# One core, attention and a feed-forward layer: the order of issue read from a written list in place of a list scheduler

## The chip, the cores and the metric

The kernel runs on one core of a Trainium2 chip. The metric is the device time of one execution in microseconds (us). Three runs of the kernel before took 973.44, 973.48 and 976.46 us. Differences within about 0.3% of the time (some 2.9 us) can't be told from no change by a few runs.

## The reference

```python
def phi(x):                       # x is q or k, scaled by 64 ** -0.25; omega is 128 x 64
    proj = einsum('bhsd,md->bhsm', x, omega)
    sq = sum(x * x, axis=-1, keepdims=True) / 2
    h = proj - sq
    return exp(h - max(h, axis=-1, keepdims=True)) / sqrt(128)
q_p, k_p = phi(q), phi(k)         # 8 batches x 8 heads, 576 rows, 64 wide
kv = einsum('bhsm,bhsd->bhmd', k_p, v)
z = sum(k_p, axis=2)
attn = einsum('bhsm,bhmd->bhsd', q_p, kv) / (einsum('bhsm,bhm->bhs', q_p, z)[..., None] + 1e-6)
x = attn as 4608 tokens x 512
h = x @ w_in                      # 512 x 2048
g = h * erf(softplus(h))
out = g @ w_out                   # 2048 x 512
```

## The kernel before

Everything is fp32. A matrix product of the feed-forward layer is three matmuls: each operand is split into a high part (`xh`, `wh`, `gh`, `th`, `bh`, ...) and a rest (`xl`, `wl`, `gl`, `tl`, `bl`, ...), and high x high, high x rest and rest x high are added up in one bank of PSUM.

The 64 heads are taken as 32 pairs. A pair is called `_b_p` (batch, pair); the steps of one are: load (`uk`, `uq`, or `x` and `y`, and `v`), square for the norm (`sqk`, `sqq`, `square`, `sumsq`, the last `s<-y` in the profile), project (banks `ppk`, `ppq`, or `pm`, `p0k`, `p0q`, `p1k`, `p1q`), maximum (`mx..`, `pm<-...`), exponential (`fk`, `fq`), sum keys with values (`kvp`, copied to `kh`), turn q round (PE transposes into `pt`, three copies `qh<-pt` called `turnhigh`; from pair 20 on through DRAM, stored as `dq` by `qstore` and read back as `qh` by four `qfetch`), multiply (`nd`), and divide (`y<-nd,rc`). The quotient `y` has one buffer. Nine or so small transfers (`yfetch`, `xs<-y` in the profile) carry it to the tokens' layout, and the next pair's `divide` may write `y` only when the last of them has landed.

The feed-forward layer runs over six groups of tokens ("supers"): two of 2 x 288 tokens with plain products, and four of 2 x 432 tokens, where the blocks are multiplied in seven products instead of eight (tables `PRODUCTS`, banks `hX`, `hY`, `hZ` for the first product and `oX`, `oY`, `oZ` for the second). Each bank is emptied several times into sums in SBUF: first by a copy (`hout` into `hs`, `oout` into `os`), then by additions (`hadd`, `oadd`, on DVE). `xsum` (`xc<-xs,..`) and `xrest` (`xl<-xc,xh`) make the operands of the first product, `gsum` (`gs<-hs`), `gate` (`hs<-gs,hs`), `high` (`th<-gs`, `bh<-hs`) and `rest` (`tl<-gs,th`) those of the second. Attention for later tokens is woven between the products of earlier ones, so that PE always has something to do.

What each step does, and what it must wait for, is written in `build`, which makes 4661 steps (`Op`). Many can go to more than one engine: copies to ACT or DVE, a gate or a rest to POOL or DVE. `Plan.order` plays the program through with estimated costs, picks for every idle engine the ready step that is due first (a table `DATES` of number and offset, indexed by the step's number, moves the due times), and returns the steps in the order in which they start, each with an engine (`o.eng`) and its buffers (`t.slot`). The loop at the end of `tile_attention_moe` emits them in that order. Each engine, and the DMA queue that SP issues, then carries out its own instructions strictly in the order in which they were emitted. All instructions have line L1523 in the profile, since one helper records them.

## Time and profile before

| | |
|---|---|
| median of 3 runs | 973.48 us |
| span of the profiled execution (first to last instruction) | 970.2 us |
| median less span: start and end around it | 3.3 us |
| PE busy, its weight loads (PEld) | 954.5 us, 903.8 us |
| DVE, ACT, POOL busy | 761.5, 625.4, 583.4 us |
| matmuls | 7868 |
| moved by DMA | 255.64 MB |

The profile is of one execution; its own total time isn't on the page, so the span stands for it and the 3.3 us are taken as fixed. Engines: PE multiplies, DVE, ACT and POOL do the elementwise work, SP issues the DMAs (rows with SPq). The kernel is one engine's work with small gaps, so what matters is where PE stands still and which engine released it. A row of a timeline that ends in "x36" is a run of 36 instructions of one kind, and its second number is the time of the whole run.

### The profile page before, as it was taken

The numbers are of one execution on the slowest core, as the hardware profiler recorded it, in microseconds if no ns is written. First come the engines' busy times: TensorE is split into PE (matmuls) and PEld (weight loads), VectorE is DVE, ScalarE is ACT, GpSimd is POOL, SyncE is SP. The second block draws the span as 40 slices with busy tenths as digits, with TensorE's granted clock in tenths as the row PEclk, the third lists the DMA queues.
The fourth block names the chain that finished last, engine by engine and source line by source line (L and its number), as shares of the span: only waits on it lengthen the run. The fifth ranks groups of instructions, "written<-read, shape, count | busy, mean of one in ns | idle before, by whom it ended". The sixth has DMA issues, their size and how long they took to land.

```text
span 970.2 us, 20988 instructions
## 1 busy us (share of the span) xinstructions
PE 954.5 (98%) x7868; PEld 903.8 (93%) x7868; DVE 761.5 (78%) x1161; ACT 625.4 (64%) x1157; POOL 583.4 (60%) x416
## 2 busy tenths in 40 slices
PE   8999999999999999999998999999999999999998
PEld 8899999999999999999998999888999999999997
DVE  6879788767777977768797879789898699668674
ACT  7869787875866766665476375666747547564650
POOL 3234534947747666748496758388686486548620
PEclk9999999999999999999999999999999999999999
DMA  8667779598897798897898999998998776697651
GB/s 250 213 212 235 236 258 329 206 329 317 309 282 227 254 322 285 257 316 232 272 316 249 385 294 322 288 301 262 292 307 248 249 243 219 215 309 220 222 184 74
DMA packets 116388, 255.64 MB, mean 263 GB/s; under 512 B 14272, under 2 KB 31168, under 8 KB 116288
## 3 DMA queue, kind: packets, MB, share of 16 engines
q1 hardware_dynamic: 116128, 254.24, 79.9%
q8 instruction: 63, 1.03, 0.4%
q14 instruction: 37, 0.30, 0.1%
q10 hardware_dynamic: 160, 0.07, 0.0%
HBM read 194.74 MB, written 50.07 MB: 252 GB/s over the span
## 4 chain that ended last, share of the span: by engine, by line
PE 56%; DMA 4%; DVE 4%; SPq 0%; ACT 0%; issue 0%; DVEq 0%; ACTq 0%
PE hX L1523 13%; PE oX L1523 11%; PE hY L1523 7%; PE o L1523 7%; PE oY L1523 5%; PE hZ L1523 4%; PE oZ L1523 3%; DMA wb<-wdc 2%; PE kvp L1523 2%; PE nd L1523 1%; PE p0k L1523 1%; PE p1k L1523 1%; DMA y<-xN 1%; DMA xs<-y 1%; DMA wb<-wdw 1%; DVE os L1523 1%
## 5 line engine op out<-in xcount | busy, mean ns | idle before, releaser
L1523 POOL TENSOR_TENSOR hs<-gs,hs 128x864 f32<-128x864 f32 (+1 forms) x56 | 111.2, 2012 | 112.0 <-ACT gs L1523 82.8
L1523 PE MATMUL o<-gh,w 128*128 128x288 f32 (+1 forms) x704 | 167.4, 317 | 0.0
L1523 PE MATMUL hX<-xh,wb 128*128 128x432 f32 x512 | 161.6, 361 | 1.8 <-DVE y L1523 1.4
L1523 PEld LDWEIGHTS o<-gh,w 128*128 128x128 f32 x704 | 120.8, 188 | 2.1
L1523 PE MATMUL h<-xh,w 128*128 128x288 f32 x512 | 110.6, 300 | 0.0
L1523 PE MATMUL o<-gl,w 128*128 128x288 f32 (+1 forms) x352 | 110.0, 312 | 0.0
L1523 PEld LDWEIGHTS hX<-xh,wb 128*128 128x128 f32 x512 | 96.1, 188 | 7.9 <-issue 1.8
L1523 ACT ACTIVATE hs<-hX 128x432 f32<-128x432 f32 x65 | 34.7, 533 | 104.0 <-PE hX L1523 103.2
L1523 PE MATMUL oX<-th,wb 128*128 128x432 f32 x312 | 97.4, 360 | 2.2 <-DVE os L1523 2.2
L1523 PE MATMUL hX<-xl,wb 128*128 128x432 f32 x256 | 91.8, 359 | 0.0
L1523 ACT ACT_TABLE_LOAD x67 | 86.0, 1283 | 2.1 <-PEq L1908 0.7
L1523 PE MATMUL hY<-xh,wb 128*128 128x432 f32 x256 | 84.0, 363 | 1.2 <-ACT fk L1523 0.4
L1523 PEld LDWEIGHTS h<-xh,w 128*128 128x128 f32 x512 | 84.2, 188 | 0.9 <-ACT fk L1523 0.2
L1523 PE MATMUL h<-xl,w 128*128 128x288 f32 x256 | 75.4, 295 | 0.0
L1523 DVE TENSOR_TENSOR os<-oX,os 128x432 f32<-128x432 f32 x86 | 50.9, 600 | 24.5 <-PE oX L1523 24.3
L1523 ACT ACTIVATE gs<-hs 128x1728 f32<-128x1728 f32 (+1 forms) x48 | 69.4, 1483 | 0.4
L1523 ACT ACTIVATE gs<-gs 128x1728 f32<-128x1728 f32 (+1 forms) x48 | 69.1, 1480 | 0.3
L1523 PEld LDWEIGHTS o<-gl,w 128*128 128x128 f32 x352 | 66.3, 188 | 0.9
L1523 PEld LDWEIGHTS oX<-th,wb 128*128 128x128 f32 x312 | 58.6, 188 | 5.9 <-DVE os L1523 2.9
L1523 POOL TENSOR_TENSOR bl<-hs,bh 128x864 fp32r<-128x864 f32 x22 | 57.5, 2634 | 0.0
L1523 PE MATMUL oX<-tl,wb 128*128 128x432 f32 x156 | 55.9, 359 | 0.0
L1523 POOL TENSOR_TENSOR tl<-gs,th 128x864 fp32r<-128x864 f32 x20 | 44.5, 2246 | 18.8 <-ACT th L1523 13.9
(162 smaller groups left out, 2699.9 us busy)
## 6 DMA issues: line engine op xcount, KB each, us to landing
wb<-wdc SPq DMA_DIRECT2D x232, 256.0 KB, 4.6
wb<-wdw SPq DMA_DIRECT2D x174, 256.0 KB, 4.8
w<-wdw SPq DMA_DIRECT2D x44, 512.0 KB, 6.1
st<-w SPq DMA_DIRECT2D x32, 512.0 KB, 5.7
wdw<-w SPq DMA_DIRECT2D x32, 512.0 KB, 4.7
wdc<-c SPq DMA_DIRECT2D x32, 512.0 KB, 5.9
x<-xR SPq DMA_DIRECT2D x20, 576.0 KB, 6.5
y<-xN SPq DMA_DIRECT2D x20, 576.0 KB, 6.3
```

Of the source, the lines that this page charges most:

```text
L1523: return tc.keep_in_program_order(method(*args, **kwargs))
```

## The change

`Plan.order` no longer schedules. It reads `ORDER`, a string of 4661 items, in the order in which they are emitted: the step's number, a letter where the step could go to several engines (T is PE, A ACT, V DVE, G POOL, S SP; without one the step takes its first option), and after a colon the buffers, one hexadecimal digit each. The costs, lags and the table `DATES` are gone. The steps, their names and what each depends on are the same 4661 as before; 390 of them change engine, and the order changes on all engines. PE has the same 7868 matmuls, SP the same 890 transfers, ACT the same 67 table loads. The other edits of the diff are new options (`TWIN`, `SUMG`, `LENT`, `BOTH` as a set), which are set so that the same steps result. All instructions now have line L1211.

```diff
-    def order(self, slots, caps):
-        ops = self.ops
...
-        for i, x in DATES:
-            ops[i].due += x
...
-                    o.eng, o.start = e, now
-                    for t in o.alloc:
-                        t.slot = free[t.pool].pop(0)
...
+    def order(self):
+
+        out, table = [], "exp"
+        for item in ORDER.split():
+            item, _, slots = item.partition(":")
+            o = self.ops[int(item.rstrip("TAVGS"))]
+            o.eng = item[-1] if item[-1] in "TAVGS" else o.opts[0][0]
+            for i, t in enumerate(o.alloc):
+                t.slot = int(slots[i], 16) if slots else 0
+            if o.eng == "A" and o.set is not None and o.set != table:
+                if o.set == "exp":
+                    out.append("table")
...
-DATES = ((0, -155.4), (1, 0.9), (2, -0.7), (4, -446.6), (5, -58.8), (6, -11.2), (7, -171), (8, -17.9),
...
+ORDER = """
...
+39:2 35A 38:1 40 42:0 47:2 49:3 41 83:3 155G 51:4 43 48V:4 52V 50A 168A 53:56 208 207:7 60:2 54V
...
+3004 3005 3103:1 3039:5 3020 3054 3040 3006 3035 3007 3041A 2882G 3016:42 3010 3036A:3 3018 3011
...
+3274 3099A:1 3275 3317:376 3333 3257A 3252A 3265 3334:0 3271 3093V 3094G 3313 3319A 3282 3318V 3283
...
-    for o in plan.order(slots, CAPS):
+    for o in plan.order():
```

The numbers that the text comes back to: 48, 50 and 52 are the three copies `qh<-pt` of the first pair (before, 48 and 50 on DVE and 52 on ACT). 3041, 3257 and 3481 are `hout` copies of banks `hY`, `hX` and `hY` (before on DVE, in the list 3041A, 3257A and 3481A).

**ACT near 30 us.** The rows of ACT before, from the exponentials of the keys of the third pair (`fk_2`) to the next q copy (`qh_2`). The name before the arrow is what is written, the last number only tells buffers apart; `uq_3` is the square for the fourth pair's q, `wt` and `w` prepare a weight, `fq_2` are the exponentials of the third pair's q.

```order
L1523 ACTIVATE fk_2_387<-ppk_2_0_333,mxk_2_351 128x128 x3
L1523 ACTIVATE fk_2_387<-ppk_2_2_356,mxk_2_351 128x128 x3
L1523 ACTIVATE fk_2_387<-ppk_2_1_347,mxk_2_351 128x128 x3
L1523 ACTIVATE uq_3_371<-uq_3_371 64x1152
L1523 ACTIVATE wt_0_2_464<-st_0_2_196 128x512
L1523 ACTIVATE w_0_1_2_194<-wt_0_1_306 128x2x256
L1523 ACTIVATE fq_2_479<-ppq_2_0_420,mxq_2_462 128x128 x3
L1523 ACTIVATE fq_2_479<-ppq_2_2_438,mxq_2_462 128x128 x3
L1523 ACTIVATE fq_2_479<-ppq_2_1_428,mxq_2_462 128x128 x3
```

The same place on ACT in the change:

```order
L1211 ACTIVATE fk_2_362<-ppk_2_2_357,mxk_2_355 128x128 x3
L1211 ACTIVATE fk_2_362<-ppk_2_1_346,mxk_2_355 128x128 x3
L1211 ACTIVATE wt_0_2_426<-st_0_2_208 128x512
L1211 ACTIVATE rc_1_435<-nd_1_0_395,eps 128x5
L1211 ACTIVATE w_0_1_2_203<-wt_0_1_299 128x2x256
L1211 ACTIVATE fq_2_450<-ppq_2_0_419,mxq_2_438 128x128 x3
L1211 ACTIVATE fq_2_450<-ppq_2_1_431,mxq_2_438 128x128 x3
L1211 ACTIVATE fq_2_450<-ppq_2_2_444,mxq_2_438 128x128 x3
```

The square of `uq_3` is no longer between the two rounds of exponentials (it is now on POOL), and a small `rc` has come in.

**DVE near 660 us.** The rows of DVE before, while PE multiplies into the `o` banks of the fourth super. `os<-oX`, `os<-oY` and `os<-oZ` empty the banks that PE waits for, `s_1` is a `sumsq` for a later pair, `xl` and `xc` are the `xrest` and `xsum` of the next super's tokens.

```order
L1523 TENSOR_TENSOR os_2_7583<-oX_2_0_8573,os_2_7583 128x432
L1523 TENSOR_TENSOR os_0_7529<-oY_2_0_8645,os_0_7529 128x432
L1523 TENSOR_REDUCE s_1_8715<-y_1_8351 128x18
L1523 TENSOR_TENSOR xl_0_8641<-xc_0_8275,xh_0_8571 128x1728
L1523 TENSOR_TENSOR os_3_7650<-oY_2_1_8722,os_3_7650 128x432
L1523 TENSOR_TENSOR os_3_7650<-oX_2_1_8581,os_3_7650 128x432
L1523 TENSOR_TENSOR xc_1_8739<-xs_1_1_7509,xs_0_1_7032 128x432
L1523 TENSOR_TENSOR xc_1_8739<-xs_1_1_7509,xc_1_8739 128x432
L1523 TENSOR_TENSOR os_1_7571<-oY_2_1_8722,os_1_7571 128x432
```

The same place on DVE in the change (`pm` and `mx` are the maximum's last steps):

```order
L1211 TENSOR_TENSOR os_2_7577<-oX_2_0_8552,os_2_7577 128x432
L1211 TENSOR_TENSOR os_1_7564<-oX_2_1_8564,os_1_7564 128x432
L1211 TENSOR_TENSOR os_3_7696<-oY_2_1_8703,os_3_7696 128x432
L1211 SCALAR_TENSOR_TENSOR pm_1_8627<-s_1_8576,pm_1_8627 128x18
L1211 SCALAR_TENSOR_TENSOR mx_1_8725<-s_1_8576,pm_1_8627 128x18
L1211 TENSOR_TENSOR xl_0_8596<-xc_0_8248,xh_0_8587 128x1728
L1211 TENSOR_TENSOR os_1_7564<-oY_2_1_8703,os_1_7564 128x432
L1211 TENSOR_TENSOR os_2_7577<-oX_2_0_8552,os_2_7577 128x432
L1211 TENSOR_TENSOR os_3_7696<-oX_2_1_8564,os_3_7696 128x432
L1211 TENSOR_TENSOR xc_1_8764<-xs_0_1_7019,xs_0_0_6988 128x432
```

The drain `os_3<-oY_2_1` now stands ahead of the long `xl`, and the `sumsq` is gone from between (it stands some twenty rows earlier).

**SP near 515 us.** The DMA issues of SP before, around the four reads of q for pair `_5_2` (`qh_2<-dq_2`) and the transfers of the quotient of pair `_5_0` (`xs_0<-y_0`); `wb` are weights, `y_0<-xN` a load.

```order
L1523 DMA wb_6965<-wdw_0_6_7_1065 128x512
L1523 DMA xs_0_0_6982<-y_0_6643 32x2x288 x2
L1523 DMA xs_0_0_6982<-y_0_6643 32x2x144
L1523 DMA qh_2_7002<-dq_2_6934 32x4x288 x4
L1523 DMA y_0_7018<-xN 128x1152
L1523 DMA wb_7025<-wdc_0_2_1_3446 128x512
L1523 DMA wb_7025<-wdc_0_3_1_3636 128x512
L1523 DMA xs_0_1_7032<-y_0_6643 32x2x144 x3
L1523 DMA xs_0_0_6982<-y_0_6643 32x2x288 x2
L1523 DMA xs_0_1_7032<-y_0_6643 32x2x144
L1523 DMA xs_0_0_6982<-y_0_6643 32x2x144 x2
L1523 DMA wb_7074<-wdc_0_2_0_3407 128x512
```

The same place on SP in the change:

```order
L1211 DMA wb_6963<-wdw_0_6_7_1064 128x512
L1211 DMA xs_0_0_6988<-y_0_6667 32x2x288
L1211 DMA xs_0_0_6988<-y_0_6667 32x2x144
L1211 DMA xs_0_0_6988<-y_0_6667 32x2x288
L1211 DMA xs_0_0_6988<-y_0_6667 32x2x144
L1211 DMA xs_0_0_6988<-y_0_6667 32x2x288
L1211 DMA y_0_7007<-xN 128x1152
L1211 DMA xs_0_0_6988<-y_0_6667 32x2x288
L1211 DMA xs_0_1_7019<-y_0_6667 32x2x144 x3
L1211 DMA wb_7033<-wdc_0_2_1_3415 128x512
L1211 DMA qh_2_7039<-dq_2_6954 32x4x288 x4
L1211 DMA xs_0_0_6988<-y_0_6667 32x2x144 x2
```

The reads of q stand behind six more of the quotient's transfers, the load of `y_0` and one weight; the last transfer of the quotient is now followed by fewer weights (one more `xs_0_1` comes behind the rows shown, ahead of the weight `wb_7074`).

## Rows read from the trace of the kernel before

**Rows 1.** The page, span and busy time of each engine.

```profile
span 970.2 us, 20988 instructions
PE 954.5 (98%) x7868; PEld 903.8 (93%) x7868; DVE 761.5 (78%) x1161; ACT 625.4 (64%) x1157; POOL 583.4 (60%) x416
```

**Rows 2.** Busy time by stretch: us; busy (instructions) per engine; clock, DMA share, GB/s.

```profile
0.00:57.00 57.00, 52.48 (x672) 48.21 (x673) 43.18 (x98) 43.77 (x137) 21.98 (x27) 1.00 0.74 215
500.00:680.00 180.00, 173.65 (x1433) 158.82 (x1433) 151.40 (x221) 113.49 (x229) 129.03 (x84) 1.00 0.93 299
```

**Rows 3.** Two windows of 25 us, columns PE, PEld, DVE, ACT, POOL as before.

```profile
650.00:675.00 25.00, 23.03 (x128) 20.89 (x127) 24.02 (x31) 17.63 (x18) 19.86 (x14) 1.00 0.91 276
875.00:900.00 25.00, 25.00 (x129) 23.93 (x128) 19.89 (x20) 10.45 (x13) 19.45 (x9) 1.00 0.71 223
```

**Rows 4.** Timeline near 15 us: start, us, engine, operation [idle before <-releaser].

```profile
13.04 1.16 ACT L1523 ACTIVATE uk<-uk 64x1152 f32<-64x1152 f32 x1 [1.16 <-DMA uk<-kT]
15.28 1.89 PE L1523 MATMUL nd<-kh,qh 128*64 128x65 f32 x35 [1.31 <-DVE qh L1523]
```

**Rows 5.** Timeline near 30 us, ACT and PE.

```profile
29.20 1.16 ACT L1523 ACTIVATE uq<-uq 64x1152 f32<-64x1152 f32 x1 [2.31 <-DMA uq<-qT]
31.41 2.43 ACT L1523 ACTIVATE fq<-ppq,mxq 128x128 f32<-128x128 f32 x9
32.34 0.55 PE L1523 MATMUL pt<-ident,fq 128*128 128x128 f32 x3 [0.63 <-ACT fq L1523]
33.37 1.17 PE L1523 MATMUL pt<-ident,fq 128*128 128x128 f32 x6 [0.49 <-ACT fq L1523]
```

**Rows 6.** Timeline near 587 us, DVE and PE.

```profile
584.78 2.19 DVE L1523 TENSOR_TENSOR gs<-hs 128x864 f32<-128x864 f32 x1
587.54 0.47 PE L1523 MATMUL hY<-xh,wb 128*128 128x432 f32 x1 [0.36 <-DVE hs L1523]
```

**Rows 7.** Timeline near 600 us, DVE, POOL and PE.

```profile
597.15 4.96 DVE L1523 TENSOR_TENSOR tl<-gs,th 128x1728 fp32r<-128x1728 f32 x1
598.11 2.19 POOL L1523 TENSOR_TENSOR gs<-hs,gs 128x432 f32<-128x432 f32 x2
609.29 0.46 PE L1523 MATMUL oX<-th,wb 128*128 128x432 f32 x1 [0.97 <-DVE os L1523]
```

**Rows 8.** Timeline from 651 to 666 us, DVE and PE.

```profile
651.40 2.08 DVE L1523 TENSOR_TENSOR tl<-gs,th 128x1728 fp32r<-128x1728 f32 x1
...
659.51 1.94 DVE L1523 TENSOR_TENSOR xl<-xc,xh 128x1728 fp32r<-128x1728 f32 x1
...
662.02 0.47 PE L1523 MATMUL oY<-bh,wb 128*128 128x432 f32 x1 [1.28 <-DVE os L1523]
...
665.07 0.46 PE L1523 MATMUL oZ<-bh,wb 128*128 128x432 f32 x1 [0.45 <-DVE os L1523]
```

**Rows 9.** Timeline from 513 to 534 us: SP's issues, PE and DVE.

```profile
513.79 3.98 SPq L1523 DMA_DIRECT2D qh<-dq  x4
...
525.43 1.22 PE L1523 MATMUL nd<-kh,qh 128*64 128x65 f32 x36
...
527.96 0.60 SPq L1523 DMA_DIRECT2D xs<-y  x1
...
531.01 0.82 DVE L1523 TENSOR_TENSOR y<-nd,rc 128x320 f32<-128x320 f32 x2 [3.90 <-DMA wb<-wdw]
...
531.65 0.44 PE L1523 MATMUL hX<-xh,wb 128*128 128x432 f32 x1 [1.42 <-DVE y L1523]
...
533.71 0.47 PE L1523 MATMUL oX<-th,wb 128*128 128x432 f32 x1 [1.23 <-DVE os L1523]
```

**Rows 10.** DMA issues from 508 to 523 us: issue, count, KB each, median us to landing.

```profile
qh<-dq SPq DMA_DIRECT2D x4, 144.0 KB, 6.1
```

**Rows 11.** Timeline of PE near 536.7 us: into the projection of x.

```profile
536.58 0.36 PE L1523 MATMUL hX<-xh,wb 128*128 128x432 f32 x1
536.87 0.37 PE L1523 MATMUL p0k<-wr,x 64*128 64x128 f32 x1
```

More of the change, by code (lines that the diff above doesn't have):

```diff
@@ L336 @@
-DATES = ((0, -155.4), (1, 0.9), (2, -0.7), (4, -446.6), (5, -58.8), (6, -11.2), (7, -171), (8, -17.9),
[439 rows of a table removed]
+    def order(self):
[9 more added lines that the diff above has]
+                    out.append("table")
+                table = o.set
+            out.append(o)
+        return out
@@ L785 @@
 ROWS = 20
-BOTH = 12
+BOTH = frozenset(range(12, 32))
+TWIN = False
+SUMG = frozenset()
+LENT = 3
 SUMA = ()
@@ L1203, in attention @@
             load(0, "q")
-        if n < BOTH:
+        if n not in BOTH:
             project(n, "q", 0.15)
         if n + 1 < N:
-            if n + 1 < BOTH:
+            if n + 1 not in BOTH:
                 load(n + 1, "k")
@@ L1218, in attention @@
         if n + 1 < N:
-            if n + 1 < BOTH:
+            if n + 1 not in BOTH:
                 project(n + 1, "k", 0.0)
@@ L1665, in project_mid, with project_rows @@
             pe.matmul(b.ap[:, :2 * P], lhsT=x.ap[:, (NC - 1) * P:], rhs=wr, start=True, stop=True)
-        def project_rows(self, banks, x, i):
-            for c in range(4):
-                for z, b in enumerate(banks):
-                    r, k = slice(z * D, (z + 1) * D), 4 * i + c
-                    pe.matmul(b.ap[:, c * P:(c + 1) * P], lhsT=x.ap[r, k * P:(k + 1) * P],
-                              rhs=wr[r, z * P:(z + 1) * P], start=True, stop=True)
+        def project_rows(self, banks, x, i, twin, head):
+            jobs = [[(banks[j][z], c, 4 * j + c) for j in range(2) for c in range(4)] for z in range(2)]
+            if twin:
+                jobs[0].insert(0, (banks[2][0], 0, NC - 1))
+                jobs[1].append((banks[2][1], 1, NC - 1))
+            cut = 4 + twin
+            for two in list(zip(*jobs))[i * cut:][:cut]:
+                for z, (b, c, k) in enumerate(two):
+                    r = slice(z * D, (z + 1) * D)
+                    m = pe.matmul(b.ap[:, c * P:(c + 1) * P], lhsT=x.ap[r, k * P:(k + 1) * P],
+                                  rhs=wr[r, z * P:(z + 1) * P], start=True, stop=True)
+                    if z and k == NC - 1:
+                        tc.add_manual_dep(m.ins, head[0].ins.name, mybir.DependencyInfo(
+                            mybir.DependencyClass.Sync, mybir.DependencyReason.DATA), reason="one bank")
         def raw(self, mid):
```

499 lines of the change are left out of this document (306 added, 193 removed), and 439 rows, old and new, of the table DATES.

## The prediction

> **What bounds the kernel now.** I read the page's head first: PE is busy 954.5 of 970.2 us, and no other engine is above 78% [rows 1]. So the time is PE's work plus its gaps, and since the change leaves PE the same 7868 matmuls, only the gaps, 970.2 - 954.5 = 15.7 us, are open to it. Busy DVE or POOL time matters only where PE waits behind it.
>
> Next I looked where the gaps lie, by stretches. Up to 57 us PE is idle 57.00 - 52.48 = 4.5 us, and from 500 to 680 us it is idle 180.00 - 173.65 = 6.35 us [rows 2]. These two stretches hold 10.9 of the 15.7 us; most of the rest lies behind the last matmul, where the last sums are stored, and that work doesn't change. A window at 875 us has no gap at all, one at 650 us has 1.97 us, and there DVE is busy 24.02 of 25 us [rows 3].
>
> Last I took the waits in the two stretches one by one, and read on the waking engine what stood ahead of the instruction that PE wanted. Near 15 us PE waits 1.31 us for a q copy; ACT, which makes the third of the three copies, is held by a square of 1.16 us [rows 4]. Near 32 us it waits 0.63 and 0.49 us for exponentials of q; ACT had first waited 2.31 us for a load and then squared it for 1.16 us, and the exponentials begin at 31.41 [rows 5]. At 587.54 PE waits 0.36 us for an `hY` drain on DVE that stands behind a gsum of 2.19 us [rows 6]; the same pattern comes twice more before 680 us, three waits in all and about 1.0 us together. At 609.29 it waits 0.97 us for an `os` drain, on a DVE that is late since a rest took 4.96 us [rows 7]. At 662.02 and 665.07 it waits 1.28 and 0.45 us for drains behind an xrest of 1.94 us [rows 8]. And near 531 us two waits of 1.42 and 1.23 us follow the divide into `y` at 531.01, which had to wait until the last `xs<-y`, issued at 527.96, had landed [rows 9].
>
> **The change part by part.** *Start.* Of the three q copies of the first pair, 50 moves to ACT, 48 and 52 are on DVE, and the square at 13.04 leaves ACT. The last copy then no longer waits for ACT's square. The nd wait can't vanish, since three copies on two engines still take two turns of 0.5 us; I take half of 1.31, 0.6 us, between 0 and 1.3. The square of `uq_3` moves to POOL, so the exponentials near 31.41 need not wait 2.31 + 1.16 us [rows 5]: both pt waits go, 1.1 us (0 if the new `rc`, which needs an nd of PE, comes late; it stands ahead of the exponentials on ACT). The first loads stand in another order, with v and a part of q ahead of two parts of the keys. The nearest row is an issue of 0.60 us [rows 9]; two of them are 0 to 1.2 us, and I take 0.3, near the lower end, since only the first pair's maxima and exponentials follow at once. Start: -0.6 - 1.1 + 0.3 = -1.4 us.
>
> *Drains.* 3041, 3257 and 3481 go from DVE to ACT and no longer stand behind a gsum: -1.0 us (0 if ACT is itself late there; it has room, 113.49 of 180 us [rows 2]). The rest of 4.96 us moves to POOL, and the wait at 609.29 behind it goes: -0.97 (0 if the maxima that stay on DVE hold it up). Near 660 us the drain `os_3<-oY_2_1` goes ahead of the xrest and the sumsq is moved twenty rows up: -1.28 - 0.45 = -1.73 (bounded by 0, as one long xrest still stands ahead of the next drain, `os_1<-oY_2_1`). Drains: -3.7 us.
>
> *The place at 531 us.* Here two things go against each other. The last transfer of the quotient is issued about two weights earlier, but PE now comes to the banks of `nd` sooner: it has 6 product matmuls and pm ahead of `p0k`, where it had 15 and pm ahead of hX. Nine matmuls at 25.00 / 129 = 0.194 us [rows 3] are 1.7 us less cover. So the first wait stays and may grow by about what the second, 1.23 us, saves. Also, the four reads of q go behind six more `xs`, a load and a weight. The six alone are 6 x 0.60 = 3.6 us, with two shorter issues some 4.4 us. Their last issue ends at 513.79 + 3.98 = 517.8 and takes 6.1 us to land [rows 9, 10], 523.9 against nd at 525.43; so 1.5 us of slack stands against 4.4, and nd may wait 2.9 us, with p0k, pm and the products queued behind it on PE. That wait overlaps the divide's, since the divide is held by the landing of `xs`, not by nd. I take 0 for the place; its ends are -2.6 (both waits gone) and +2.9.
>
> *Refilling PE.* The first matmul after each wait takes 0.46 or 0.47 us where one in the stream takes 0.36 [rows 7, 8, 11]; eight waits fewer are 8 x 0.1 = -0.8 us.
>
> *Switching PE.* The row-wise projections now come in 24 groups in place of 21. Going in costs 536.87 - 536.58 = 0.29 us from start to start in place of 0.194 [rows 11, 3]; with as much on the way out it is 0.2, for three groups +0.6 us.
>
> *The other moves.* 390 steps change engine. Between 500 and 680 us ten steps go from POOL to DVE (three rests and two gates among them) and seven back, and sixteen each way between DVE and ACT. A rest takes DVE 2.08 to 4.96 us [rows 8, 7]. Net four rests and gates more on DVE are 8.3 us at the shorter price; three gsums at 2.19 us [rows 6] leave it, 6.6 us. With the small steps, most of which cancel, I take 2 to 6 us more, so up to 157 of 180. PE waits for none of it as long as the drains are first in line. I cost it at nothing; what it costs when that cover is gone is the second rival.
>
> Sum: -1.4 - 3.7 + 0 - 0.8 + 0.6 = -5.3 us. Against the profiled execution that is a span of 970.2 - 5.3 = 964.9; with the 3.3 us around it, which put it at the median of 973.5, 968.2 us.
>
> **Rivals.** *The waits only move.* Every drain has a neighbour that is nearly as late: in the window at 650 us DVE has 0.98 us of 25 free [rows 3], and a reordering on a full engine makes another bank late. For it speaks that DVE gets more work in that very stretch, against it that ACT and POOL have room (113.49 and 129.03 of 180 us [rows 2]) and take the drains. If all of the stretch's 6.35 us stay and only the start's 1.4 us comes, the time is 973.5 - 1.4 + 0.6 = 972.7, at most 975.6 with the 2.9 us of nd: no difference that can be measured (970.6 to 976.4).
>
> *DVE becomes the bound from 500 to 680 us (slower).* A rest on DVE took 4.96 us at 597.15, while POOL worked beside it from 598.11, and 2.08 us at 651.40 [rows 7, 8]: the same instruction, 2.88 us apart. If the five rests and gates that move to DVE there all meet POOL, that is 5 x 2.88 = 14.4 us more; with the 2 to 6 us, 168 to 172 of the 173.65 us that PE works. DVE is then as full everywhere as it is now in the window at 650 us, where PE loses 1.97 us in 25 [rows 3]. Over 180 us that is 14.2 us in place of 6.35, so 973.5 + 7.8 - 1.4 = 979.9 us. It decides from about 24 of 25 busy DVE microseconds on; below that the drains find room. Against it: POOL is busy 129.03 of 180 us there [rows 2], and drops work that goes to DVE, so not every one of the five meets it. The Trainium skill has a rule that speaks for this rival (SBUF - State Buffer, Who interferes with whom): a DVE instruction with two inputs in SBUF contends with a GpSimd instruction that reads SBUF, since the second input comes by a shared port, and what holds the shared pair can make the other block. The trace agrees with it as far as 4.96 against 2.08 us go, and by it the sum would be 979.9, where the shorter price gives 968.2.
>
> *More is won than the waits that I counted.* If the place at 531 us loses both waits (-2.6) and the start its whole 1.31, it is 968.2 - 2.6 - 0.7 = 964.9; with every gap of both stretches but the 1.2 us before the first matmul gone, 973.5 - 10.9 + 1.2 - 0.8 = 963.0. The Trainium skill holds (Perfetto Trace Analysis, Identifying the Most-Contended Engine) that matmul busy time is a poor measure of the room that PE has, and that the share of its weight loads should be read. The gapless window has a share of 23.93 / 25.00 = 0.957 [rows 3], so 903.8 us of loads [rows 1] would fit into 944 us, an estimate of 26 us of room in place of 15.7. Were a third of that taken, as 5.3 is of 15.7, it would be 964.7.
>
> **How the numbers follow.** The forecast has a chance of 0.50, from 966 to 971 by its own terms (half the drains' 3.7 lost, or half the place's 2.6 won, and a little over). More won: 0.12, 963 to 965. The waits only move: 0.20, 971 to 976. DVE bound: 0.18, 976 to 982. Faster by over 0.3% is the forecast but for its upper edge, and the larger gain: 0.60. Within 0.3%: 0.21. Slower: 0.19. The range from 963 to 978 leaves out the upper half of the slower case and a thin edge below, under 2 in 10.
>
> **What would show it.** In the changed kernel: no wait for `pt` near 32 us and a shorter one for the first `nd`; no PE wait for an `hs` drain near 587, 633 and 675 us, none for `os` near 609 and 662; PE idle from 500 to 680 us near 3 us; near 525 to 531 one wait, at `nd` or `p0k`, in place of two. The forecast is wrong if DVE is at 24 of 25 us in several windows of that stretch, if rests on DVE take near 5 us again and again, or if PE waits appear in stretches where I named none.

## The result, and the profile after

The changed kernel takes 984.6 us (median of 6 runs, 983.86 to 987.46), the kernel before 976.88 us in the same comparison (6 runs, 973.44 to 980.98). The ratio is 1.0082, with an interval of 1.0055 to 1.011: slower by 8 us where I forecast 968.2. The 973.48 us that I started from were three of the shorter runs of the kernel before; its medians in the later comparisons lie between 976.07 and 978.65. One of the six executions of `e2_engines_only` below took 1505.52 us at a granted clock of 0.576, a slower state, and is left out there.

The 3.3 us that I took as start and end around the span are not that. In the 73 later executions of the kernel before whose span is on record, the time is 1.65 to 1.75 us above it. So the profiled span of 970.2 belongs to an execution of some 972 us, shorter than each of those 73 (972.42 to 983.89 us). The profiled execution of the change took 984.5 us, its median.

The page of the profiled execution after, span and busy time [rows 1]:

```profile
span 982.4 us, 20966 instructions
PE 959.3 (98%) x7868; PEld 904.6 (92%) x7868; DVE 766.4 (78%) x1163; ACT 624.3 (64%) x1156; POOL 560.7 (57%) x407
```

The span grew by 12.2 us, of which some 4.5 are that short execution before, since the medians differ by 7.7. PE's gaps went from 15.7 to 982.4 - 959.3 = 23.1 us, which is 7.4 of them, and PE's busy time grew by 4.8 us with the same matmuls. DVE's busy time grew by 4.9 us at the same share of 78%; ACT and POOL have less to do.

The stretches of after [rows 2], columns us, PE, PEld, DVE, ACT, POOL, clock, DMA share, GB/s:

```profile
0.00:57.00 57.00, 51.18 (x673) 47.57 (x674) 42.16 (x97) 45.48 (x140) 23.71 (x27) 1.00 0.81 229
57.00:325.00 268.00, 265.88 (x2706) 258.90 (x2705) 209.05 (x367) 197.45 (x421) 139.97 (x124) 1.00 0.78 268
500.00:680.00 180.00, 172.49 (x1409) 156.50 (x1408) 148.66 (x224) 113.14 (x225) 120.81 (x77) 0.99 0.91 293
680.00:981.00 301.00, 295.66 (x1747) 279.29 (x1745) 226.44 (x278) 160.64 (x185) 153.41 (x88) 1.00 0.70 232
```

One of these stretches of the kernel before, which the text ahead doesn't show:

```profile
57.00:325.00 268.00, 268.00 (x2729) 262.23 (x2730) 209.93 (x376) 200.22 (x422) 150.38 (x129) 1.00 0.81 273
```

There is now idle time where there was none: 2.12 us from 57 to 325 us. From 500 to 680 us PE is idle 7.51 us where I forecast about 3 and before had 6.35.

PE's waits in after: waiting bank, releaser, us in total, times, longest.

```profile
PE oX L1211 <- DVE os L1211: 3.3, 3, 2.4
PE hX L1211 <- DVE gs L1211: 2.2, 1, 2.2
PE hX L1211 <- DVE hs L1211: 1.4, 2, 1.2
PE nd L1211 <- DMA qh<-dq: 1.2, 1, 1.2
...
PE ppk L1211 <- ACT uk L1211: 1.1, 1, 1.1
PE kvp L1211 <- PE ppq L1211: 0.9, 1, 0.9
PE ppq L1211 <- ACT uq L1211: 0.9, 1, 0.9
PE oX L1211 <- DMA wb<-wdc: 0.9, 1, 0.9
PE ppq L1211 <- ACT fk L1211: 0.8, 1, 0.8
```

What I said would go is gone: there is no wait for `pt`, and between 553.83 and 692 us, where the change runs some 8 to 11 us later than before, PE has only two waits left, 2.40 us at 630.78 and 0.34 at 669.68; neither is one of those that I named. The first `nd`, at 15.98, waits 0.22 us in place of 1.31 [rows 4]:

```profile
15.98 1.50 PE L1211 MATMUL nd<-kh,qh 128*64 128x65 f32 x36 [0.22 <-DVE qh L1211]
```

In place of these waits there are others, elsewhere. To see where they cost, I set the start of the n-th matmul of after against the n-th of before (us later than before, at numbers 200, 500, 700, 4800, 5100, 5300, 6300 and the last; the numbers mark the same amount of PE's work, which is good to some 1 to 2 us where the order on PE differs):

```
time in before   21    45    61    506   543   567   691   end
after           +1.3  -1.4  +2.0  +5.5  +4.5  +9.8  +9.2  +12.2
```

So against this one execution, at 45 us the change is ahead by the 1.4 us that I forecast for the start. It loses 3.4 us in the next 16 us, 3.5 more up to 506, 5.3 between 543 and 567, and 3.0 behind 691. How far such differences repeat from one execution to the next is read below, where more traces of the same lists are at hand.

**The largest piece, 543 to 567 us.** SP's issues in after, then the weight's transfer (KB each, us to landing), PE, and two windows of 5 us:

```profile
533.60 0.38 SPq L1211 DMA_DIRECT2D dq<-fq  x1
...
537.02 0.53 SPq L1211 DMA_DIRECT2D out<-os  x1
540.98 1.27 SPq L1211 DMA_DIRECT2D qh<-dq  x3
...
543.29 0.85 SPq L1211 DMA_DIRECT2D wb<-wdc  x2
...
544.79 1.31 SPq L1211 DMA_DIRECT2D wb<-wdw  x2
```

```profile
wb<-wdw SPq DMA_DIRECT2D x1, 256.0 KB, 8.9
```

```profile
550.21 0.43 PE L1211 MATMUL hY<-xh,wb 128*128 128x432 f32 x1 [0.66 <-DVE hs L1211]
...
553.83 0.44 PE L1211 MATMUL hX<-xh,wb 128*128 128x432 f32 x1 [2.20 <-DVE gs L1211]
...
555.14 0.56 PE L1211 MATMUL hX<-xh,wb 128*128 128x432 f32 x1
555.50 0.56 PE L1211 MATMUL hY<-xh,wb 128*128 128x432 f32 x1
```

```profile
545.00:550.00 5.00, 4.54 (x25) 3.89 (x23) 4.86 (x9) 4.41 (x8) 4.01 (x2) 1.00 0.94 299
550.00:555.00 5.00, 2.59 (x11) 2.19 (x12) 4.26 (x5) 2.80 (x11) 5.00 (x4) 0.96 1.06 405
555.00:560.00 5.00, 5.00 (x20) 4.67 (x20) 1.39 (x2) 2.37 (x7) 2.46 (x3) 0.70 0.79 300
```

SP stands from about 537.5 to 540.98, for 3.4 us: the reads of `dq` may start only when the `qstore` of 533.60 has landed, 7.3 us after its issue. Two weights are queued behind them, and a load (`x`) and a store (`out`) besides. The second is issued at 544.79 and lands 8.9 us later, at 553.69, with the DMA share at 1.06; PE starts with it at 553.83. The row names a gsum of DVE as the releaser, which neither reads nor writes what this matmul uses; the landing of the transfer fits. The run `m1` below has the change's list at this place, and there the rows of the same two matmuls name the weights:

```profile
549.70 0.43 PE L1204 MATMUL hY<-xh,wb 128*128 128x432 f32 x1 [0.41 <-DMA wb<-wdc]
552.74 0.43 PE L1204 MATMUL hX<-xh,wb 128*128 128x432 f32 x1 [1.63 <-DMA wb<-wdw]
```

Then PE's clock falls: in the window from 555 us the granted clock is 0.70, part of it at the lower level of 1.2 GHz, and the matmuls start 0.36 us apart (555.14, 555.50) where one in the stream takes 0.194. Nine such steps, from 554.78 to 558.01, are 9 x (0.36 - 0.194) = 1.5 us. PE counts as busy in that time, so this is a third of the 4.8 us by which its busy time grew; all other windows of 20 us have a clock of 1.00.

**The longest wait, 630.78.** DVE, then PE, in after:

```profile
629.60 0.61 DVE L1211 TENSOR_TENSOR xc<-xs,xs 128x432 f32<-128x432 f32 x1 [3.48 <-DMA xs<-y]
630.12 0.60 DVE L1211 TENSOR_TENSOR os<-oX,os 128x432 f32<-128x432 f32 x1
```

```profile
630.78 0.46 PE L1211 MATMUL oX<-th,wb 128*128 128x432 f32 x1 [2.40 <-DVE os L1211]
```

The drain that PE wants (630.12) is behind an `xsum` that waits 3.48 us for a transfer of `y`.

I followed fifteen of PE's waits, of 0.3 to 2.4 us, back step by step, always to what was last. Eleven of them, 12.3 us together, end at a transfer that landed late: it brought PE's own operand, or an instruction that needed it stood ahead of the one that PE wanted. Of the eleven I had costed only the 1.22 us of `nd` at 532 us as a wait.

### The profile page after: what moved, and what is told of

It reads as the page before. It is cut to its first block, busy times and chain, and to the rows that moved or that the text cites. A ratio compares the mean times of both kernels' runs of the same rounds, so it can differ in the third digit from the quotient of the medians.

```text
span 982.4 us, 20966 instructions
## 1 busy us (share of the span) xinstructions
PE 959.3 (98%) x7868; PEld 904.6 (92%) x7868; DVE 766.4 (78%) x1163; ACT 624.3 (64%) x1156; POOL 560.7 (57%) x407
## 3 DMA queue, kind: packets, MB, share of 16 engines
q8 instruction: 63, 1.03, 0.5%
## 4 chain that ended last, share of the span: by engine, by line
PE 79%; DMA 8%; DVE 7%; SPq 3%; ACT 1%; issue 1%; POOL 0%; DVEq 0%; POOLq 0%; ACTq 0%
PE o L1211 15%; PE hX L1211 13%; PE h L1211 10%; PE oX L1211 9%; PE hY L1211 7%; PE oY L1211 4%; PE hZ L1211 3%; PE kvp L1211 3%; SPq L1211 3%; PE nd L1211 3%; DMA st<-w 2%; PE oZ L1211 2%; DMA xs<-y 2%; DMA wb<-wdc 2%; PE pt L1211 2%; PE ppk L1211 2%
## 5 line engine op out<-in xcount | busy, mean ns | idle before, releaser
L1211 POOL TENSOR_TENSOR hs<-gs,hs 128x864 f32<-128x864 f32 (+1 forms) x48 | 104.2, 2196 | 113.6 <-ACT gs L1211 103.8
L1211 PE MATMUL hX<-xh,wb 128*128 128x432 f32 x512 | 165.0, 365 | 3.7 <-DVE gs L1211 2.2
L1211 PE MATMUL o<-gh,w 128*128 128x288 f32 (+1 forms) x704 | 166.5, 316 | 0.0
L1211 PEld LDWEIGHTS o<-gh,w 128*128 128x128 f32 x704 | 120.6, 188 | 2.2
L1211 PE MATMUL h<-xh,w 128*128 128x288 f32 x512 | 111.5, 300 | 0.7 <-POOL xh L1211 0.6
L1211 PE MATMUL o<-gl,w 128*128 128x288 f32 (+1 forms) x352 | 109.8, 312 | 0.0
L1211 PEld LDWEIGHTS hX<-xh,wb 128*128 128x128 f32 x512 | 96.3, 188 | 11.7 <-DVE hs L1211 2.8
L1211 PE MATMUL oX<-th,wb 128*128 128x432 f32 x312 | 99.9, 362 | 4.2 <-DVE os L1211 3.3
L1211 ACT ACTIVATE hs<-hX 128x432 f32<-128x432 f32 x68 | 36.0, 533 | 90.8 <-PE hX L1211 90.6
L1211 PE MATMUL hX<-xl,wb 128*128 128x432 f32 x256 | 92.1, 360 | 0.6 <-DVE xl L1211 0.6
L1211 PEld LDWEIGHTS h<-xh,w 128*128 128x128 f32 x512 | 84.6, 188 | 2.1 <-POOL xh L1211 0.8
L1211 PE MATMUL hY<-xh,wb 128*128 128x432 f32 x256 | 84.6, 364 | 0.9 <-DVE hs L1211 0.7
L1211 PE MATMUL h<-xl,w 128*128 128x288 f32 x256 | 75.8, 296 | 0.7 <-DVE xl L1211 0.7
L1211 ACT ACTIVATE gs<-gs 128x1728 f32<-128x1728 f32 (+1 forms) x48 | 69.5, 1480 | 0.3
L1211 ACT ACTIVATE gs<-hs 128x1728 f32<-128x1728 f32 (+1 forms) x48 | 69.3, 1481 | 0.3
L1211 DVE TENSOR_TENSOR os<-oX,os 128x432 f32<-128x432 f32 x86 | 51.2, 601 | 22.9 <-PE oX L1211 21.8
L1211 PEld LDWEIGHTS o<-gl,w 128*128 128x128 f32 x352 | 66.3, 188 | 0.8
L1211 PEld LDWEIGHTS oX<-th,wb 128*128 128x128 f32 x312 | 58.6, 188 | 8.8 <-DVE os L1211 5.8
L1211 POOL TENSOR_TENSOR y<-y 128x288 f32<-128x288 f32 x40 | 30.9, 798 | 54.4 <-DMA y<-xN 26.0
L1211 PE MATMUL oX<-tl,wb 128*128 128x432 f32 x156 | 55.8, 358 | 0.0
L1211 POOL TENSOR_TENSOR tl<-gs,th 128x864 fp32r<-128x864 f32 x20 | 43.4, 2187 | 16.6 <-ACT th L1211 13.5
```

What stands on the lines that cost most here:

```text
L1211: return tc.keep_in_program_order(method(*args, **kwargs))
```

## The experiments

The lists name a step by its number, with the engine's letter; a line of a diff headed by an engine shows the order in that engine's queue.

**Which half of the change: order, engines, or SP?** `e1_order_only` has the order of the change, but the 390 steps on the engines of before; `e2_engines_only` the reverse; `e3_sp_only` is the kernel before with SP's issues in the order of the change.

```diff
 e1, among 390 steps of the changed list
-3041A 3257A 3481A 71G 130G
+3041V 3257V 3481V 71A 130A
 e2, among 390 steps of the list of before
-3041V 3257V 3481V 71A 130A
+3041A 3257A 3481A 71G 130G
 e3, S, the first of 890 issues
-0 2 1 16 17 18 3 31 45 32 69 206 294 153 167 213
+0 3 16 1 2 31 18 17 294 45 69 32 153 167 206 213
```

> The order and the buffers of the change, but all 390 steps that changed engine put back on the engine they had before. Theory (late transfers): 10 of the 15 longer PE waits of the change go back to a transfer that lands late, so the order makes the loss and this stays near the change, 981 to 987 us, 0.5 to 1.2% slower than before. Rival (DVE becomes the bound): the loss goes with the engines, 973 to 978 us, within 0.3% of before.

> The order of before, with the 390 steps on the engines that the change gives them. Theory (late transfers): within 0.3% of before, or a little faster, 971 to 979 us, since SP's order is that of before. Rival (DVE becomes the bound): 982 to 987 us, 0.6 to 1.1% slower.

> The kernel before with one engine's order taken from the change: the 890 transfers that SP issues; all other engines keep order and step placement of before. Theory (late transfers): much of the loss comes with it, 3 to 8 us, 979 to 985 us. Rival (SP's order is right, the other engines' orders ask for the data too early): within 0.3% of before.

Measured: 1027.99 us (ratio 1.0503, 1.0469 to 1.0536), 996.37 us (median of five; 1.0176, 1.014 to 1.0213) and 1039.52 us (1.0627, 1.059 to 1.0663). The largest waits of e1, then of e3:

```profile
PE oX L1204 <- DVE os L1204: 16.9, 3, 15.6
```

```profile
PE hX L1204 <- ACT hs L1204: 18.0, 1, 18.0
PE hY L1204 <- DMA wb<-wdc: 9.8, 5, 4.7
```

Each half alone is worse than both together. A list's order fits its own engines and its own queue; half of it makes, in e1 and e3, stalls of 15 to 18 us that neither kernel has. So these runs don't divide the 8 us. What follows is that placement, order and SP's order have to be taken as one, and that the loss must be looked for by place in the program.

**The first loads.** `e4_first_loads` is the change with the first 16 issues of SP as before. My reason: the waits at `ppk` and `ppq` of the first pair, 1.1 and 0.9 us, which before didn't have, follow on the new order of the loads.

```diff
 S
-0 3 16 1 2 31 18 17 294 45 69 32 153 167 206 213
+0 2 1 16 17 18 3 31 45 32 69 206 294 153 167 213
```

> The change with SP's first 16 issues in the order of before (the three parts of the first keys first, then q, then v). Theory: the PE waits of 1.1 and 0.9 us at 6.5 and 9.7 us go, 1.5 to 2 us less than the change, 982.5 to 983 us where the change takes 984.6. Rival: other waits in the first 60 us take their place and the time is that of the change within 0.5 us.

Measured: 991.7 us, 1.0122 (1.0084 to 1.0161), against the change's 1.0082: no gain. The wait at 9.66 us is gone, that at 6.47 us is still 0.95, and a new one of 1.49 us comes at 22.95. In its one trace it is 0.8 us behind the changed kernel at 13 us and 3.6 at 45. So the order of the first loads is not by itself what puts the change 1.8 us behind at 13 us.

**The place at 550 us, and all places.** `f1_sp_weights` issues the first late weight ahead of the reads of `dq` and the second right behind them; the load `x` and the store `out` that stood ahead go behind both. `f_all` does that, and puts six more steps behind what PE waits for: the `xsum` 3445, the `gsum` 4423, the `xhigh` 2581, the `gate` 1096 and two preparations of weights (207, 376) on ACT; and it brings a weight's second half (3920) forward on SP.

```diff
 f1, S
-2798 2800 2799 2891 2801 2857 2858 2781 2865 2866
+2857 2858 2798 2800 2799 2801 2865 2866 2891 2781
 f_all, with f1, V
-3445 3185 3177 3225 3193
+3185 3177 3225 3193 3445
-4423 4495 4487 4503
+4495 4487 4503 4423
-2581 2528
+2528 2581
-1096 1161 1192
+1161 1192 1096
 A
-207 44
+44 207
-376 164
+164 376
 S
-3919 3927 3928 3935 3790 3791 3936 3792 3793 3920
+3919 3920 3927 3928 3935 3790 3791 3936 3792 3793
```

> The change with five of SP's issues near 541 us moved: the two transfers of the weight wb127 go ahead of the four reads of q (SP stands idle there until the store of q has landed), the last read of q goes ahead of a load, and the two transfers of wb128 right behind it. Theory (weights held up in SP's queue behind the round trip of q through DRAM): the waits of 0.66 and 2.20 us at 550.2 and 553.8 us go, and with them the 18 matmuls that take 0.36 us from start to start in place of 0.197 (2.9 us): 4 to 6 us less than the change. Rival (the DMA engines are full there, share 0.94 to 1.06, and another transfer lands later by as much): within 1 us of the change.

> The change with the five moves at 541 us and seven more, each of one instruction on its own engine past its neighbours, at places where PE waits: an xsum and an xhigh that wait for a transfer go behind the drains that queue behind them (DVE, 630 and 477 us), a gsum and a gate behind drains (DVE, 928 and 217 us), two steps of the weight preparation that wait for a load behind exponentials (ACT, 20 and 44 us), and the second half of a weight next to its first (SP, 767 us). Theory (the loss is a dozen local waits, most of them for transfers): 8 to 11 us less than the change, so level with before. Rival (the waits only move to the next neighbour): at most 3 us less than f1.

Measured: f1 986.67 us, 1.0094 (1.0061 to 1.0127); f_all 982.81 us, 1.0073 (1.0049 to 1.0096). The windows of f1 at the same place:

```profile
550.00:555.00 5.00, 4.97 (x26) 4.43 (x25) 4.97 (x6) 4.99 (x18) 5.00 (x3) 1.00 1.03 405
555.00:560.00 5.00, 5.00 (x36) 4.54 (x36) 4.57 (x7) 3.94 (x7) 4.46 (x5) 1.00 1.03 398
```

The cause at this place is shown: with the weights in time PE is full and the clock stays at 1.00, though the DMA share is still 1.03 and DVE is busier (4.97 of 5.00 us). SP stands in f1 too, until 541.58, for PE. What changed is the order of the transfers: the two halves of `wb<-wdc` land in 4.8 us (median) in place of 7.6, those of `wb<-wdw` in 6.0 where the first took 8.9. (The nine slow steps of the trace are 18 in the expectation, and cost half of what stands there.) From 543 to 567 us f1 loses 0.7 us where the change lost 5.3. But 3.3 of these 4.6 us are lost again by 691 us, where the change lost nothing, and the time is no better than the change's, as the rival said. Two of the new waits:

```profile
628.29 0.46 PE L1204 MATMUL oX<-th,wb 128*128 128x432 f32 x1 [1.71 <-DVE os L1204]
...
674.42 0.46 PE L1204 MATMUL oZ<-bh,wb 128*128 128x432 f32 x1 [1.76 <-DVE os L1204]
```

`f_all` is 6.0 us slower than before where the change was 7.7, and the intervals overlap. That one late place, or all of these together, carries the whole loss is refuted.

**Weights whose halves are fetched apart.** In the change 71 of 203 pairs of half weights have other issues between them, before 20. `h_halves` puts each second half right behind the first.

```diff
 S, one of the pairs that stand apart
-3919 3927 3928 3935 3790 3791 3936 3792 3793 3920
+3919 3920 3927 3928 3935 3790 3791 3936 3792 3793
```

> The change with SP's order altered in one respect only: of the weights that are fetched in two transfers, the second is put right behind the first wherever other issues stood between (62 moves; in the order of before 20 of the 203 pairs are apart, by 5 issues at most, in the change 71, by up to 20). Theory (second halves that land late make PE wait): 3 to 8 us less than the change. Rival (the place of the halves was right, and what is pushed back lands late instead): no less than the change, up to 10 us more.

Measured: 987.57 us, 1.0107 (1.0082 to 1.0133): not faster than the change. The theory falls.

**The first or the second part of the list.** `m1_before_then_after` follows before to about 380 us and the change from there, `m2_after_then_before` the reverse.

```diff
 m1: all 4661 steps, each with the engine of the list that it is taken from
+the first 2060 steps of the list of before, then the rest in the order of the change
 m2
+the first 2080 steps of the list of the change, then the rest in the order of before
```

> The order, engines and buffers of before up to about 380 us, those of the change from there on (19 buffers had to be numbered otherwise at the seam). By the two traces the change loses some 3.5 us up to there and some 8.7 us after it. Theory (waits spread over the whole program, most of them behind 380 us): 6 to 9 us slower than before. Rival (the loss is the change's start): within 2 us of before.

> The change up to about 380 us, before from there on (28 buffers numbered otherwise). Theory: 2 to 5 us slower than before. Rival (the loss is the change's start): 7 to 9 us slower, as the change.

Measured: m1 986.33 us, 1.0095 (1.0068 to 1.0121); m2 984.01 us, 1.0078 (1.005 to 1.0107). Both parts are slow by themselves, 9.3 and 7.6 us, and the sum of 17 us is twice what the whole change loses, so some of each is the joint. m2 comes out as its rival said and m1 as its theory, so neither account fits both. In m2 most of the loss comes at one place, from 45 to 61 us (ACT, then PE):

```profile
46.33 0.64 ACT L1204 ACTIVATE wt<-st 128x512 f32<-128x512 f32 x1 [4.93 <-DMA st<-w]
```

```profile
47.82 2.93 PE L1204 MATMUL ppq<-wqk,uq 128*128 128x128 f32 x12 [4.08 <-ACT fk L1204]
```

A preparation of a weight, which waits 4.93 us for its load, stands on ACT ahead of the exponentials. The same wait of PE is 0.8 us in the profiled execution of the change, 2.7 in f1, 2.8 in f_all and 3.8 in h_halves, all with the same issues on SP up to there. `f_all` had moved the step, 376, behind the first of three exponentials only.

**Behind all the exponentials there.** `f2_weights_44` is f_all with these steps on ACT behind all three exponentials, and two on DVE behind the maximum.

```diff
 A
-164 376 165 379 166
+164 165 166 376 379
 V
-377 162 378 163
+162 163 377 378
```

> The changed kernel with the repairs of f_all, and near 44 us the preparation of two weights (two steps each on DVE and ACT) issued behind the exponentials that PE waits for. If the wait near 47 us (0.8 us in the profiled execution of the change, 2.7 to 4.1 us in four others with the same start) comes from ACT and DVE standing in line for a weight that has not landed: no wait above 0.5 us there, 0.8 to 3 us less than f_all, ratio to the kernel before 1.003 to 1.006. Rival: the exponentials wait for their own loads, and the time is that of f_all, ratio 1.006 to 1.009.

Measured: 982.57 us, 1.0075 (1.0052 to 1.0098). The wait for `fk` is gone from the trace, and a wait of `kvp` of 1.47 us comes right behind it:

```profile
47.56 1.38 PE L1204 MATMUL kvp<-v,fk 128*64 128x130 f32 x36 [1.47 <-issue]
```

The time is that of f_all, as the rival said. The trace of f2 is 2.6 us shorter than that of f_all at the end, but the medians, 982.57 and 982.81, don't show it.

**Only the parts that I counted as gains.** `g_all` is the kernel before with the same waits removed in its own way, each step on its own engine: three gsums behind the drains at 587, 633 and 675 us, two drains ahead of the `xrest` at 662 us, the quotient's last transfer two weights earlier, one square behind the exponentials. `g2_start` only moves two squares from ACT to POOL as the change does; `g3_start_drains` adds three gsums and the quotient's transfer.

```diff
 g_all, V
-2879 3041 3049 3052
+3041 3049 3052 2879
-3091 3257 3260
+3257 3260 3091
-3299 3481 3492
+3481 3492 3299
-3456 3369 3393
+3369 3393 3456
 S
-2833 2834 2696
+2696 2833 2834
 A
-130 226 217 112 114 113
+226 217 112 114 113 130
 g2, in the list of before
-71A
+71G
-130A
+130G
```

> The kernel before with seven moves of one instruction on its own engine, at the waits from which the prediction worked out its gain: three gsums behind the drains that they held up (587, 633, 675 us), two drains ahead of an xrest (660 us), the last transfer of the quotient ahead of two weights on SP (527 us), the square of uq_3 behind the exponentials on ACT (29 us). If the waits removed are worth what the prediction put on them: 3 to 4 us less than before, a ratio of 0.996 to 0.997. Rival (each wait has a neighbour nearly as late): within 0.1% of before.

> The kernel before with one thing of the change only: the squares `sqk` of pair _0_2 and `sqq` of pair _0_3 go from ACT to POOL, and all else is issued as before. Theory A (the start's gain is real and the rest of the change loses it): the first nd wait of the profiled executions of before's start (1.31 to 4.8 us near 15 us) falls below 0.5 us and the pt waits near 32 us (1.1 us together) go; nothing later is touched, so all of it stays: 2 to 4 us less than the kernel before, ratio 0.996 to 0.998. Rival B (waits only move): another load or POOL's square is late next, PE gets back less than 1 us, ratio 0.999 to 1.001.

> The same as g2_start, and in the middle three gsums of DVE issued behind the drains that stood behind them (near 587, 633 and 675 us), and one fetch of y earlier. Theory A: a further 1 to 3 us less than g2_start, ratio 0.994 to 0.997. Rival B (between 500 and 680 us the transfers set the pace and a reordering there only moves waits): the same as g2_start within 0.1%.

Measured: g_all 975.9 us, 0.999 (0.9977 to 1.0003); g2 975.31 us, 0.9989 (0.9968 to 1.0009); g3 975.6 us, 0.9988 (0.9971 to 1.0005). All three are about a part in a thousand below before, which the intervals don't tell from no change. The waits that g_all goes for stand in my sum with 1.1 + 1.0 + 1.73 = 3.8 us, and measure as 1 us, by the interval as 2.2 at most. The rest that moves to POOL (0.97) and the copy 50 on ACT are in none of the three. Two places show how a wait comes back. In g2, POOL, DVE and PE at 14 us:

```profile
13.97 2.43 POOL L1203 TENSOR_TENSOR uk<-uk 64x576 f32<-64x576 f32 x2
```

```profile
14.20 1.21 DVE L1203 TENSOR_SCALAR st<-st 128x512 int32<-128x512 int32 x1 [1.26 <-DMA st<-w]
15.32 1.01 DVE L1203 COPY qh<-pt 128x384 f32<-128x384 f32 x2
```

```profile
15.92 1.73 PE L1203 MATMUL nd<-kh,qh 128*64 128x65 f32 x36 [1.93 <-DVE qh L1203]
```

ACT makes its copy early now (14.03), but the square on POOL lies beside DVE's work on a weight, which takes 1.21 us in place of 0.43 at the same place before. DVE's two copies come 0.65 us later, and PE waits 1.93 us in place of 1.31. The Trainium skill has a rule for this (SBUF - State Buffer, Who interferes with whom): an instruction like `tensor_scalar`, which may use DVE's second pair of ports, then excludes GpSimd from it, and the one that comes second waits. The pair of 1.21 and 0.43 us agrees with it; which mode the instruction ran in no run here shows.

In g_all, the two drains near 662 us go ahead of the xrest, and now the next drains stand behind it and two xsums (DVE, then PE):

```profile
663.41 2.89 DVE L1203 TENSOR_TENSOR xl<-xc,xh 128x1728 fp32r<-128x1728 f32 x1
```

```profile
667.91 0.46 PE L1203 MATMUL oZ<-bh,wb 128*128 128x432 f32 x1 [2.37 <-DVE os L1203]
```

In the kernel before the wait at this matmul is 0.45 us [rows 8], and of the 2.3 us that g_all wins from 506 to 543, 2.1 are lost again by 691. g3 leaves the place as it is and loses 4.0 us from 616 to 691 us all the same, so its trace says nothing on the drains.

**Are the transfers short from 500 to 680 us?** `x_mid` is the kernel before with 12 extra copies of 256 KB, each issued right behind a weight between 504 and 662 us; `x_late` has the same 12 between 738 and 895 us.

```diff
+    extra = [2762, 2834, 2866, 2970, 3038, 3077, 3170, 3238, 3277, 3371, 3403, 3501]
     for o in plan.order():
...
+        if o != "table" and o.id in extra:
+            scr = dr.tile([P, 512], I32, name=f"scr{o.id}", tag=f"scr{o.id}")
+            sp.dma_start(scr, w1[0, 0].bitcast(I32)[:, :512])
```

> The kernel before, with 12 more transfers of 256 KB from DRAM to DRAM (no engine waits for them), each issued by SP behind a weight between 504 and 662 us. They are 3.1 MB, about 10 us of the 300 GB/s that this stretch moves. Theory (waits removed between 500 and 680 us come back since the DMA engines are full there): 5 to 10 us slower than before. Rival (DVE is what is short there, and DMA only looks busy): at most 1.5 us slower.

> The same 12 transfers, but between 738 and 895 us, where the DMA engines are busy about 0.7 of the time. Theory and rival alike: at most 1 us slower than before, since there is room. If this is as slow as the run with the transfers in the middle, it is SP's 12 more issues and not the full DMA engines that cost.

Measured: x_mid 980.19 us, 1.0045 (1.0026 to 1.0064); x_late 977.77 us, 1.0005 (0.9988 to 1.0022). The same bytes cost 3.6 us in the middle, less than the theory's 5 to 10 and more than the rival's 1.5; later the 1.2 us between the medians lie within the interval. The stretches that took the copies, in x_mid and then in x_late:

```profile
504.00:662.00 158.00, 152.87 (x1318) 139.99 (x1317) 127.05 (x190) 95.37 (x200) 103.68 (x67) 0.98 0.96 315
```

```profile
738.00:895.00 157.00, 156.59 (x905) 148.25 (x904) 119.34 (x148) 94.21 (x103) 95.45 (x55) 1.00 0.79 256
```

At a share of 0.96 more transfers cost time, at 0.79 they hardly do. So between 500 and 680 us the transfers have a part in the time. That what is fetched earlier there delays something else follows from it as a likely reason, and no run shows it by itself.

The shifts of the experiments against before's profiled execution, as in the table above (one execution of each):

```
time in before   21    45    61    506   543   567   691   end
f1              +1.7  -0.8  +4.8  +7.5  +6.0  +6.7  +10.0 +13.4
f_all           +1.1  -1.6  +4.3  +7.8  +6.7  +7.4  +10.5 +11.1
f2              +1.4  -1.0  +2.8  +5.3  +4.3  +5.0  +7.9  +8.5
m2              +0.5  -2.0  +5.8  +7.8  +8.8  +8.8  +8.9  +8.8
g_all           +2.7  +2.1  +2.1  +2.9  +0.6  +0.6  +2.7  +2.7
g2              +0.4  -0.5  -0.6  -0.6  +1.8  +1.8  +3.6  +3.6
g3              +0.8  +0.1  +0.1  -0.4  -3.5  -3.5  -0.7  -0.8
m1              +0.9  +2.5  +2.5  +5.2  +4.2  +7.2  +11.6 +15.0
x_late          +5.5  +7.6  +7.5  +8.2  +10.3 +10.3 +10.5 +11.0
```

x_late has before's list unaltered up to 738 us, and is 10.5 us later than before's profiled execution at 691: so much can lie between two executions of one list. Most of it arises up to 45 us and from 506 to 543 (2.1 us, and 2.4 in g2 with the same list there); g2 loses 1.8 more from 567 to 691. Elsewhere the two lists differ in every trace. From 61 to 506 us the change, f1, f_all and f2 lose 2.5 to 3.5 us, while x_late, g2, g3 and g_all lie between -0.5 and +0.8. From 543 to 567 us the change loses 5.3 and m1, the same list there, 3.0; x_late, g2 and m2, with before's, lose nothing. Behind 691 us the change, f1 and m1 lose 3.0 to 3.4, and g2, g3 and m2 at most 0.1. There f_all and f2 lose only 0.6, and they lack the waits of 0.85 us at 782.31 and 1.18 at 928.39 that the change has: what stood ahead of PE's steps at these two places is shown as a cause too.

## Why the prediction was wrong, point by point

**What bounds the kernel** held: PE's work and its gaps, and the gaps before lay where I said. But I took "only the gaps are open" to mean that they can only shrink. In the change they grew by 7.4 us, and PE's own busy time, which I took as fixed, by 4.8 us: 1.5 of it is the lower clock behind the stall at 550 us. Of the lines of PE, `hX<-xh,wb` (161.6 to 165.0 us) and `oX<-th,wb` (97.4 to 99.9) grew most; that this is PE stopping and starting anew at these banks is my reading, which no run isolates. The rule of the Trainium skill that I set beside it (Perfetto Trace Analysis, Identifying the Most-Contended Engine), that matmul busy time is a poor measure of PE's room, agrees with the trace so far: 954.5 and 959.3 us stand for the same 7868 matmuls.

**Start, -1.4.** At 45 us the trace shows just that, -1.4 us, but by luck: with before's list m1 stands at +2.5 there and x_late at +7.6, and the first `nd` wait, 1.31 us in my rows, is 4.78 in x_late. And it comes by other terms: the change is 1.8 us behind at 13 us, where my sum has +0.3 for the first loads (by e4 their order is not the whole reason), and `nd`, `pt` and the rest give 3.2 back. The step stopped there. At 45 us an ACT step for a weight stands ahead of exponentials; with the waits at 59 and 60 us behind it (0.60 and 0.68), 3.4 us are lost by 61 us. By itself the square's move (g2) gave nothing that can be told from no change; in g2's trace the copies on DVE take the place of the one on ACT as the late ones.

**Drains, -3.7.** All the waits named are gone. From 567 to 691 us the change is 0.6 us better than before, not 3.7: waits of 2.40 us at 630.78 and 0.34 at 669.68 took the place. The size of even this is open, since before's list is 0.1 to 1.8 us slower there in m2, x_late and g2 than in the execution that I started from, and the change's list in m1 loses 4.4. It is what the rival "the waits only move" says of a drain, and g_all shows it without the rest of the change.

**The place at 531 us, 0.** It went about as costed: the divide's two waits (2.65 us) are gone and `nd` waits 1.22 for the reads of q that are issued behind the quotient's transfers; from 506 to 543 us the change wins 1.0 us. I took the 6.1 us to landing, a median of four, for the last read; that one lands 5.2 us after 517.46, so `nd` had 2.8 us of slack and not 1.5.

**Refilling, -0.8, and switching, +0.6,** can't be seen apart in the traces; both are below what one execution differs from the next.

**"The other moves. ... PE waits for none of it as long as the drains are first in line. I cost it at nothing."** This is the step that failed. I weighed the 390 moved steps as load on engines and asked if DVE would be full. DVE has 148.66 us in that stretch, less than the 151.40 before, and up to 675 us no window of 25 us has over 22.88. Its rests `tl` take 1.95 to 2.38 us where before had up to 4.96; the two rests `bl` and a gate that ran beside POOL's work take 2.71, 2.92 and 3.26. So the slower rival, DVE as the bound, did not happen: its price per rest is there, but about a third of what it stood with (0.8 to 1.3 us over 1.95, in place of 2.88). What happened is in the queues: SP, ACT and DVE carry out their lists strictly in order, and a step that waits for a transfer holds what is behind it. The wait at 630.78, that at 550 to 554 and that at 45 us are of this kind; a full engine is not the reason: at 550 us DVE was busier in f1, without the wait. I had this price in hand: I wrote of reads of q behind six more transfers, but looked at SP's queue only at 515 us and not at its other 870 issues. Had I listed, for each step that waits for a transfer, what stands behind it in the new lists, the places at 45, 550 and 630 us would have been candidates with a price: a landing of 5 to 9 us less what covers it. Put at nothing, this term measures 5.3 us from 543 to 567 us alone in the profiled execution, and f1 shows its cause.

**The base.** Of the miss of 16.4 us, 3.4 are the starting point, 973.48 against the 976.88 of the comparison (976.07 in the one with most runs, 23), 5.3 the gain that did not come, and 7.7 the loss. The term of 3.3 us around the span is 1.65 to 1.75 in the runs, since the profiled execution was shorter than the median that I put it at.

**What stays open.** The places that I could name (f_all, f2) hold perhaps 2 of the 8 us. Both parts of the list are slow when joined to the other list (m1, m2), and a joint has its own price. So I take the rest to be spread over many short waits, of which the trace shows those of 0.2 to 1.2 us in stretches that had none before; no run shows a single cause for it, and none rules one out. A version that beats both kernels was not found; g_all, g2 and g3 are level with before.

## What to carry to other kernels

On an engine without free gaps a wait removed is worth its time only if the next step in that queue is early; here 3.8 us of waits brought about 1, which the interval doesn't tell from nothing. Count on a fraction, and try the one edit by itself. When a change rewrites an order, read its queues, not its loads: for each step that waits for a transfer, what stands behind it, and how late it may land where the DMA share is near 1. Take more than one trace of the kernel before, too: at 691 us two executions of one list were 10.5 us apart. An order fits its own engines and its own queue; with the engines or SP's queue of the other list (e1, e2, e3) it was worse than either kernel.
